# Regrouping the small products of the late steps in a fused linear-attention and feed-forward kernel

## The chip, the core and the metric

The kernel is one program on one core of a Trainium2 chip. Times are device microseconds (us) of that core. The engines are named as in the profile: PE (matrix products; PEld is its weight load), DVE (VectorE), ACT (ScalarE), POOL (GpSimd) and SP, which here issues DMAs.

## The reference, cut to what matters

An attention block with a decaying state runs over 768 tokens for 4 sequences of 8 heads of width 48; its output, as 3072 rows of 384, goes through a feed-forward block of width 2048. Everything is float32.

```python
for t in range(S):
    cur = einsum('bhd,bhe->bhde', u[None] * kt, vt)
    y[:, :, t] = einsum('bhd,bhde->bhe', rt, state + cur)
    state = wt[:, :, :, None] * state + einsum('bhd,bhe->bhde', kt, vt)
...
h = x @ w_in
sp = maximum(h, 0) + log1p(exp(-abs(h)))
return (h * erf(sp)) @ w_out
```

## The kernel before, in words

**Steps.** The kernel takes the tokens in 12 steps, numbered 0 to 11: six chunks of 128 tokens by two halves of the batch. A step holds 2 sequences by 8 heads, and a chunk of 128 tokens is two halves of 64 (`HC`). Steps 0 to 4 are handled by `attend_first` and `attend`. Steps 5 to 11, the late steps (`s > DIRECT`, `DIRECT` is 4), are handled by `attend_late` (L693), and the change is there.

**What a late step computes.** Inside a half of 64 tokens the attention is a triangle of 64 by 64 per head, called `own`. Its blocks of 16 by 16 on the diagonal come from element-wise products and sums on DVE and POOL, made one step ahead by the generator `prepare` (L354). The rest comes from PE at levels 5 and 6, which join blocks of 16 into 32 and of 32 into 64. What came before the half comes from a state of 48 by 48 per head, which decays from half to half.

**Small products.** These attention products use at most 64 of the 128 rows and columns of the PE array. In a late step `s` they are:

- `from_own` (L575, matmuls at L584), in two calls: `own` of step `s-1` times the values, added into the tile `y`;
- `level_products` (L540, matmuls at L552) for level 5 and then for level 6, into the tile `pp0`;
- `through_state` (L598, matmuls at L610): the state of step `s-1`, added into `y`. ACT then copies `y` to `xT`, the input of the feed-forward block, partly by way of `y3` and a DMA;
- `spread_blocks` (L667, matmuls at L672): turns the decays between blocks of 16 (`over_blocks`), which ACT copies to `few` and two DMAs bring to `spread`;
- `state_part` (L650, matmuls at L659): keys times values, which DVE adds to the state. The keys are first multiplied by `spread` (L718), here called the fade of the keys.

**Large products.** `hidden` (L994, matmuls at L1027) is the first feed-forward product, of step `s-1`. `project` (L1044, L1059) and `project_fast` (L1127, L1142) are the second one, of step `s-3`. Each is a generator that emits one piece at a time. Between them stand softplus and erf on ACT (L983, L987, each behind a table load) and a multiplication on DVE (L992). `blend` (L1102) makes the sums that `project_fast` needs out of copies that ACT makes (L1100).

**Order.** Everything from the first step on is written in the order in which each engine executes it; no scheduler moves it. [...] A late step calls `run(stage, following)` at fixed places, and each stage plays a string of tokens (`USUAL`, with two other sets in `LATE` for steps 5 and 11): `P` and `H` are one piece of `project` or `hidden`; `s`, `ey`, `ep`, `m` are softplus, erf into the tile `y` or into `pp1`, and the multiplication of one chunk; `k..`, `S..` are copies and sums for `blend`; `F` lets `prepare` of the next step go on to its next `yield`; `G` sends a weight sum to POOL; `w` sends one of the DVE sums that the last two steps need.

**`prepare` of a late step.** POOL makes products of decays (L402) and `over_blocks` (L424 to L426). DVE makes the near terms of distances 1 to 4 (L463, L467) and sums them (`sum_up`, L453). POOL then makes the terms of distances 5 to 15 (the first of them goes into the room that holds distance 1, so it can start only once that was summed). DVE sums these. Keys and sums are written to DRAM and read back in another layout (`k_blocks` L499, `by_blocks` L501, `by_tokens` L503, `kT` L509), all issued on SP in this order. DVE scales r and k at L328 (`scale`), and at last writes `own` from `by_tokens` (L514), which the next step's first PE instruction reads.

**The queue at the end of a late step.** On DVE, the state sums are `middle` (L736) and, after a POOL product `faded[1]` (L739), `S_next` (L743).

Of the kernel before, what the change touches and what calls it, by code (L numbers as in the profile page):

```python
# [11 lines left out]
FP32 = mybir.dt.float32  # L12
# [5 lines left out]
P = 128  # L18
FAST = 3
EP = 64  # L20
HC = 64
# [40 lines left out]
def kernel(  # L62
# [50 lines left out]
    over_blocks = const.tile([P, C // NEAR, JP], FP32, name="over_blocks")  # L113
# [90 lines left out]
    def near_log(s):  # L204
        return NEAR_LOG - (s == DIRECT)
# [148 lines left out]
    def prepare(s):  # L354
# [61 lines left out]
        if s == DIRECT:  # L416
            yield
        else:
            half = view(tots[NEAR_LOG + 1], 1, [[2, NC], [C >> NEAR_LOG + 1, JP]])
            quarter, last = (  # L420
                view(tots[NEAR_LOG], n, [[4, NC], [C >> NEAR_LOG, JP]]) for n in (1, 3)
            )
            to = over_blocks[:].rearrange("p (h b) n -> p b h n", h=NC)
            nc.gpsimd.tensor_mul(to[:, 0], quarter, half)  # L424
            nc.gpsimd.tensor_copy(out=to[:, 1], in_=half)
            nc.gpsimd.tensor_copy(out=to[:, 2], in_=last)  # L426
            yield
# [84 lines left out]
        scale(s, near_log(s))  # L512
        nb = HC // NEAR
# [153 lines left out]
    def spread_blocks(s, pp):  # L667


        n = D // 2  # L670
        for e in range(NE):
            nc.tensor.matmul(  # L672
                pp[:EP, e, 0:2, HC // 2 : HC // 2 + n],
                lhsT=over_blocks[rows(e)].rearrange("p b n -> p (b n)"),
                rhs=ident[rows(e), rows(e)], start=True, stop=True,
            )
        few = att.tile([EP, NE * 2, n], FP32, name="few", bufs=1)
        nc.scalar.copy(
            few[:].rearrange("p (e i) d -> p e i d", e=NE),
            pp[:EP, :, 0:2, HC // 2 : HC // 2 + n],  # L680
        )
# [3 lines left out]
            in_=few[:].rearrange("p i d -> p (i d)"),  # L685
# [7 lines left out]
    def attend_late(s, run):  # L693
# [10 lines left out]
        take_level(own, pp, LOG - 1)  # L704
        run("front", None)
        if before:
            from_own(before, ready[before][0], 0)
            through_state(before, xTs[before])
            if s + 1 < n_steps:
                load_step(s + 1)  # L710
        following = prepare(s + 1) if s + 1 < n_steps else iter(())
# [3 lines left out]
        run("near", None)  # L715
        next(following, None)
        kT = kTs[s]
        nc.vector.tensor_mul(  # L718
            kT[:].rearrange("p (e n) d -> p n e d", e=NE),
            kT[:].rearrange("p (e n) d -> p n e d", e=NE), spread[s][:],  # L720
        )
        run(0, following)

        pp = products([P, NE, JP, HC], 0)
        level_products(pp, RK, LOG)
        if s + 1 < n_steps:
            spread_blocks(s + 1, pp)
        take_level(own, pp, LOG)
        scale(s, LOG)
        run(1, following)  # L730
        ps = products([P, NC, JP, HC], 0)
        ps = [[ps[:, h]] * NE for h in range(NC)]
        state_part(s, kT, ps)
        run(2, following)
        for e in range(NE):
            nc.vector.tensor_add(middle[rows(e)], faded[0][rows(e)], ps[0][e][rows(e), :, :D])  # L736
        run(3, following)
        if s < n_steps - SPC:
            nc.gpsimd.tensor_mul(  # L739
# [4 lines left out]
        run(4, following)  # L744
# [575 lines left out]
    def in_order(s, k):  # L1320
# [3 lines left out]
        for what in order[k]:  # L1324
# [11 lines left out]
            "s ey", "m", "s ep m P P s ey m P P P", "s P F ep m P F P k22y k11p F", "S1",  # L1336
            "S2 S3 H k12y S4 H F", "s H ep m H H F G s H H H ep",
        ),
        n_steps - 1: (
            "s P", "m w", "ey P m s P P ep P", "m P P", "", "", ""  # L1340
# [3 lines left out]
        "s P", "m", "ey P m s P P ep P", "m k22y P F P k11p F F", "S1", "S2 S3 H k12y S4 H F",  # L1344
        "s H ey m H H F s H ep H H",
# [67 lines left out]
    with tc.manual_schedule(  # L1413
# [77 lines left out]
        run_late(s - 1, "S Q w w w")  # L1491
# [105 lines left out]
```

## Time and profile before

| what | value |
|---|---|
| median of 3 runs | 583.61 us (583.38 to 589.66) |
| profiled execution, its own time | 586.88 us |
| span in its profile | 585.1 us |
| PE busy / DVE / ACT / POOL | 576.4 / 454.7 / 355.6 / 274.1 us |
| late steps 6 to 10, from one first small product to the next | 44.75, 44.50, 44.50, 44.50, 44.49 us |
| granted PE clock | 0.999 |

A busy time of PE counts overlapping matmuls and modelled ends, so that 99% busy isn't 99% of its peak. In the views of the timeline a line is: start in us, length in us, engine, source line, operation, tiles written and read, shape, number of instructions, and in brackets how long the engine stood idle before it and what released it. Each float32 matmul of the program shows as two records on PE. The first small product of step s (L584 for s from 6 to 11) is called A(s) in this text.

### The profile page before, as it was taken

The page shows a single profiled execution, that of the slowest core. Times are in us where ns is not written, and L with a number is a line of the kernel's source. Part 1 is how long each engine was busy: PE and PEld are TensorE (multiplying, and loading weights), DVE is VectorE, ACT ScalarE, POOL GpSimd, SP SyncE. Part 2 cuts the span into 40 slices and gives each one's busy share as a digit, 9 for nine tenths or more (in the row PEclk, how much of TensorE's full clock was granted, in tenths as well). Part 3 has the DMA queues.
Part 4 walks back from the last instruction along what each step waited for, and adds up shares of the span by engine and source line. Part 5 has one row for each costly group of instructions (what it writes and reads, how often), then busy time and mean ns, then how long its engine had stood idle before and what let it go on. Part 6 is the DMA issues. An engine that isn't in the chain of part 4 may idle for free.

```text
span 585.1 us, 16663 instructions
## 1 busy us (share of the span) xinstructions
PE 576.4 (99%) x7240; PEld 495.1 (85%) x7240; DVE 454.7 (78%) x558; ACT 355.6 (61%) x478; POOL 274.1 (47%) x313
## 2 busy tenths in 40 slices
PE   8899999999999999999999999999999999999997
PEld 6588887688668758998898898898898899988997
DVE  6776886999996899799799799799799637256630
ACT  3658877644544598756766666665765771387700
POOL 4557391702398469659459459449549200000000
PEclk9999999999999999999999999999999999999999
DMA  8587571440433414334334334334331301000000
GB/s 269 177 273 281 201 235 44 183 154 10 145 95 116 117 55 156 63 116 165 74 111 169 74 108 172 75 108 136 74 108 55 74 8 36 2 0 2 28 27 29
DMA packets 54082, 63.25 MB, mean 108 GB/s; under 512 B 35160, under 2 KB 40568, under 8 KB 52984
## 3 DMA queue, kind: packets, MB, share of 16 engines
q1 hardware_dynamic: 53624, 61.98, 33.4%
q8 instruction: 57, 0.93, 0.6%
q10 hardware_dynamic: 384, 0.20, 0.1%
q14 instruction: 17, 0.14, 0.1%
HBM read 52.39 MB, written 8.69 MB: 104 GB/s over the span
## 4 chain that ended last, share of the span: by engine, by line
PE 95%; DVE 3%; issue 1%; ACT 0%; POOL 0%; DVEq 0%; POOLq 0%
PE m L1027 36%; PE m L1142 28%; PE m L1059 8%; PE pp L552 6%; PE pp L1230 4%; PE y L1230 2%; PE y L584 2%; PE pp L659 2%; PE y L610 2%; PE m L862 1%; PE pp L871 1%; PE pp L938 1%; DVE in L328 1%; DVE words L467 1%; PE pp L1142 0%
## 5 line engine op out<-in xcount | busy, mean ns | idle before, releaser
L1027 PE MATMUL m<-xT,w_in_sb 128*128 128x256 f32 x960 | 215.3, 382 | 0.1
L1027 PEld LDWEIGHTS m<-xT,w_in_sb 128*128 128x128 f32 x960 | 179.9, 190 | 26.2 <-issue 1.0
L328 DVE TENSOR_TENSOR in<-in,tot_sb 128x1024 f32<-128x1024 f32 (+1 forms) x55 | 75.3, 1369 | 16.5 <-PE pp L552 13.2
L463 POOL TENSOR_TENSOR rk<-words 128x528 f32<-128x528 f32 (+3 forms) x28 | 42.5, 1517 | 91.2 <-DVE sums L453 80.7
L1036 ACT COPY h<-m 128x512 f32<-128x512 f32 x80 | 46.4, 579 | 57.6 <-PE m L1027 57.5
L467 POOL TENSOR_TENSOR words<-words,rest 128x528 f32<-128x528 f32 (+10 forms) x77 | 78.1, 1015 | 6.0
L1059 PE MATMUL m<-w_out_sb,h 128*128 128x384 f32 x192 | 64.3, 491 | 0.0
L1059 PEld LDWEIGHTS m<-w_out_sb,h 128*128 128x128 f32 x192 | 35.7, 190 | 23.5
L1142 PE MATMUL m<-mixed,h 128*128 128x192 f32 x256 | 45.6, 331 | 0.0
L1142 PE MATMUL m<-w_out_sb,h 128*128 128x192 f32 x256 | 44.8, 329 | 0.0
L552 PEld LDWEIGHTS pp<-in 48*64 48x64 f32 (+1 forms) x2368 | 33.4, 126 | 12.0 <-issue 6.2
L1142 PEld LDWEIGHTS m<-mixed,h 128*128 128x128 f32 x256 | 41.4, 190 | 0.9
L1142 PEld LDWEIGHTS m<-w_out_sb,h 128*128 128x128 f32 x256 | 41.6, 190 | 0.3
L1142 PE MATMUL m<-w_out_sb,room 128*128 128x192 f32 x240 | 41.5, 326 | 0.0
L983 ACT ACT_TABLE_LOAD x30 | 38.5, 1283 | 2.7 <-issue 2.2
L987 ACT ACT_TABLE_LOAD x30 | 38.5, 1283 | 1.5 <-DVE room L1125 1.1
L1142 PEld LDWEIGHTS m<-w_out_sb,room 128*128 128x128 f32 x240 | 39.4, 190 | 0.0
L402 POOL TENSOR_TENSOR tot_sb<-tot_sb 128x256 f32<-128x256 f32 (+4 forms) x50 | 36.2, 724 | 3.8
L552 PE MATMUL pp<-in 48*64 48x32 f32 (+1 forms) x2368 | 37.3, 212 | 0.6 <-DVE in L328 0.5
L463 POOL TENSOR_TENSOR words<-words 128x336 f32<-128x336 f32 (+6 forms) x49 | 35.3, 720 | 3.8
L453 DVE TENSOR_REDUCE sums<-rk 128x14 f32<-128x672 f32 (+9 forms) x54 | 34.7, 701 | 0.0
L453 DVE TENSOR_REDUCE sums<-words 128x6 f32<-128x288 f32 (+8 forms) x66 | 26.9, 464 | 3.9 <-POOL words L463 3.6
(198 smaller groups left out, 951.5 us busy)
## 6 DMA issues: line engine op xcount, KB each, us to landing
in<-in_rkw SPq DMA_DIRECT2D x8, 1024.0 KB, 5.1
words<-in_moe_w_in SPq DMA_DIRECT2D x16, 384.0 KB, 5.4
words<-in_moe_w_out SPq DMA_DIRECT2D x16, 384.0 KB, 4.7
words<-in_rk_rows SPq DMA_DIRECT2D x8, 768.0 KB, 5.6
w<-in_rkw SPq DMA_DIRECT2D x11, 512.0 KB
v<-in_v SPq DMA_DIRECT2D x12, 384.0 KB, 5.6
out<-o SPq DMA_DIRECT2D x23, 192.0 KB, 2.4
in<-in_rkw SPq DMA_DIRECT2D x7, 512.0 KB, 5.7
```

What stands on the lines that cost most here:

```text
L328: nc.vector.tensor_mul(halves, halves, view(tots[level - 1], 0, [[1, n], [2, nb], [0, half]]))
L402: nc.gpsimd.tensor_mul(new, pair[:, :, 0], pair[:, :, 1])
L453: nc.vector.tensor_reduce(out=view(sums[:], n, [[near * (NEAR + 1), NEAR // near], [NEAR + 1, near - n]]), in_=terms[n], axis=mybir.AxisLi ...
L463: engine.tensor_mul(terms[n], r[:, :, n:], k[:, :, : near - n])
L467: engine.tensor_mul(k[:, :, :m], k[:, :, :m], w[:, :, n : n + m])
L552: nc.tensor.matmul(to, lhsT=rk(1, n)[rows(e), s0 : s0 + m], rhs=right, start=True, stop=True,)
L983: nc.scalar.activation(sp_room, chunks[0], AF.Softplus)
L987: nc.scalar.activation(at, sp_room, AF.Erf)
L1027: nc.tensor.matmul(ps[:, ff, :], lhsT=w_in_sb[:, g * FG + f + ff, kk * P : (kk + 1) * P], rhs=xT[:, kk, :], start=kk == 0, stop=kk == KT - 1,)
L1036: nc.scalar.copy(h[:, f : f + FT, :], ps[:])
L1059: nc.tensor.matmul(ps[j][:], lhsT=gs[g][:, f, j * C : (j + 1) * C], rhs=w_out_sb[:, g * FG + f, :], start=g + f == 0, stop=g == NG - 1 and ...
L1142: nc.tensor.matmul(to, lhsT=a[:, f], rhs=b[:, f], start=start and f == 0, stop=f == FG - 1, skip_group_check=True,)
```

## The change

**Grouping.** In a late step `s` the small products stand in two groups. The first is unchanged: `from_own(…, 1)` and level 5. The second begins after the stages front and near and holds `from_own(…, 0)`, `through_state`, level 6 and `state_part`, with nothing between them. `state_part` writes to `pp1` where it wrote to `pp0`.

**The key fade.** `fade_keys(s + 1)` is called at the end of step `s`, behind the write of `own`; for step 5 it is called in the step itself, ahead of the stage front.

**The state sums.** They follow the near terms that DVE makes, ahead of the first `sum_up`; `faded[1]` is made on DVE.

**The spread.** `spread_blocks` stands behind stage 0 and is one matmul on the whole array (128 rows, 128 columns of weights, 96 moving columns), for which `over_blocks` has twice its size, the second half staying at 1.0. Step 4 keeps the former form for the spread of step 5.

**Tokens.** In the usual steps the stage near is empty, its `m` being moved to the end of the last stage, and `prepare` has one more `yield`, ahead of the write of `own`, with one more `F` behind that `m`. The other two sets change alike; step 5 keeps its `m` in the stage near. The stage near itself is played ahead of the second group and of `prepare`, where it was behind them.

```diff
@@ prepare
         scale(s, near_log(s))
+        yield
         nb = HC // NEAR
@@ spread_blocks
+        few = att.tile([EP, NE, D], FP32, name="few", bufs=1)
+        if s > DIRECT + 1:
+            got = products([P, NE * JP * HC], 0)[:, : NE * D].rearrange("p (e d) -> p e d", e=NE)
+            nc.tensor.matmul(
+                got, lhsT=over_blocks[:].rearrange("p i b n -> p (i b n)"),
+                rhs=ident[:].rearrange("p (e m) -> p e m", e=NE)[:, :, :D],
+                start=True, stop=True,
+            )
+            nc.scalar.copy(few[:], got[:EP])
...
@@ attend_late
         take_level(own, pp, LOG - 1)
+        if s == DIRECT + 1:
+            fade_keys(s)
         run("front", None)
+        run("near", None)
         if before:
             from_own(before, ready[before][0], 0)
             through_state(before, xTs[before])
             if s + 1 < n_steps:
                 load_step(s + 1)
+        pp = products([P, NE, JP, HC], 0)
+        level_products(pp, RK, LOG)
+        ps = products([P, NC, JP, HC], 1)
+        ps = [[ps[:, h]] * NE for h in range(NC)]
+        state_part(s, kTs[s], ps)
+        take_level(own, pp, LOG)
         following = prepare(s + 1) if s + 1 < n_steps else iter(())
         next(following, None)
         nc.gpsimd.tensor_mul(faded[0][:], S[:], ends[:, :, 0:1].to_broadcast([P, JP, D]))
         next(following, None)
-        run("near", None)
-        next(following, None)
-        kT = kTs[s]
-        nc.vector.tensor_mul(
-            kT[:].rearrange("p (e n) d -> p n e d", e=NE),
-            kT[:].rearrange("p (e n) d -> p n e d", e=NE), spread[s][:],
-        )
-        run(0, following)
-
-        pp = products([P, NE, JP, HC], 0)
-        level_products(pp, RK, LOG)
-        if s + 1 < n_steps:
-            spread_blocks(s + 1, pp)
-        take_level(own, pp, LOG)
-        scale(s, LOG)
-        run(1, following)
-        ps = products([P, NC, JP, HC], 0)
-        ps = [[ps[:, h]] * NE for h in range(NC)]
-        state_part(s, kT, ps)
-        run(2, following)
         for e in range(NE):
             nc.vector.tensor_add(middle[rows(e)], faded[0][rows(e)], ps[0][e][rows(e), :, :D])
-        run(3, following)
         if s < n_steps - SPC:
-            nc.gpsimd.tensor_mul(
+            nc.vector.tensor_mul(
                 faded[1][:], middle[:], ends[:, :, 1:2].to_broadcast([P, JP, D])
             )
             for e in range(NE):
                 nc.vector.tensor_add(S_next[rows(e)], faded[1][rows(e)], ps[1][e][rows(e), :, :D])
-        run(4, following)
+        next(following, None)
+        scale(s, LOG)
+        run(0, following)
+        if s + 1 < n_steps:
+            spread_blocks(s + 1)
+        for n in range(1, 5):
+            run(n, following)
+        for _ in following:
+            pass
+        if s + 1 < n_steps:
+            fade_keys(s + 1)
+
+    def fade_keys(s):
+
+        kT = kTs[s][:].rearrange("p (e n) d -> p n e d", e=NE)
+        nc.vector.tensor_mul(kT, kT, spread[s][:])
@@ tokens
     LATE = {
         DIRECT + 1: (
-            "s ey", "m", "s ep m P P s ey m P P P", "s P F ep m P F P k22y k11p F", "S1",
-            "S2 S3 H k12y S4 H F", "s H ep m H H F G s H H H ep",
+            "s ey", "m", "s ey m P P s ep m P P P", "s P F ep m P F P k22y k11p F", "S1",
+            "S2 S3 H k12y S4 H F", "s H ep m H H F G s H ep H H m F",
         ),
         n_steps - 1: (
-            "s P", "m w", "ey P m s P P ep P", "m P P", "", "", ""
+            "s P", "", "ey P m s P P ep P", "m P P", "", "", ""
         ),
     }
     USUAL = (
-        "s P", "m", "ey P m s P P ep P", "m k22y P F P k11p F F", "S1", "S2 S3 H k12y S4 H F",
-        "s H ey m H H F s H ep H H",
+        "s P", "", "ey P m s P P ep P", "m k22y P F P k11p F F", "S1", "S2 S3 H k12y S4 H F",
+        "s H ey m H H F s H ep H H m F",
     )
...
-        run_late(s - 1, "S Q w w w")
+        run_late(s - 1, "S Q w w w w")
```

More of the change, by code (lines that the diff above doesn't have):

```diff
@@ L111 @@
     seen = const.tile([P, NE * NP * NC], FP32, name="seen")
-    over_blocks = const.tile([P, C // NEAR, JP], FP32, name="over_blocks")
+    over_blocks = const.tile([P, 2, C // NEAR, JP], FP32, name="over_blocks")
     u_sb = const.tile([P, NP], FP32, name="u_sb")
@@ L422, in prepare @@
             )
-            to = over_blocks[:].rearrange("p (h b) n -> p b h n", h=NC)
+            to = over_blocks[:, 0].rearrange("p (h b) n -> p b h n", h=NC)
             nc.gpsimd.tensor_mul(to[:, 0], quarter, half)
@@ L665, in state_part, with spread_blocks @@
                     )
-    def spread_blocks(s, pp):
-        n = D // 2
-        for e in range(NE):
+    def spread_blocks(s, pp=None):
+        few = att.tile([EP, NE, D], FP32, name="few", bufs=1)
+        if s > DIRECT + 1:
+            got = products([P, NE * JP * HC], 0)[:, : NE * D].rearrange("p (e d) -> p e d", e=NE)
             nc.tensor.matmul(
-                pp[:EP, e, 0:2, HC // 2 : HC // 2 + n],
-                lhsT=over_blocks[rows(e)].rearrange("p b n -> p (b n)"),
-                rhs=ident[rows(e), rows(e)], start=True, stop=True,
-            )
[L677 to L680, printed above, removed]
-        )
+                got, lhsT=over_blocks[:].rearrange("p i b n -> p (i b n)"),
+                rhs=ident[:].rearrange("p (e m) -> p e m", e=NE)[:, :, :D],
+                start=True, stop=True,
+            )
+            nc.scalar.copy(few[:], got[:EP])
+        else:
+            n = D // 2
+            got = pp[:EP, :, 0:2, HC // 2 : HC // 2 + n]
+            for e in range(NE):
+                nc.tensor.matmul(
+                    got[:, e], lhsT=over_blocks[rows(e), 0].rearrange("p b n -> p (b n)"),
+                    rhs=ident[rows(e), rows(e)], start=True, stop=True,
+                )
+            nc.scalar.copy(few[:].rearrange("p e (i d) -> p e i d", i=2), got)
         g_rows = dram.tile([C // NEAR, JP * NE * D], FP32, name="g_rows")
@@ L684, in spread_blocks @@
             out=g_rows[:].rearrange("b (n d) -> (b n) d", n=JP),
-            in_=few[:].rearrange("p i d -> p (i d)"),
+            in_=few[:].rearrange("p e d -> p (e d)"),
         )
@@ L714, in attend_late @@
         next(following, None)
-        run("near", None)
-        next(following, None)
-        kT = kTs[s]
-        nc.vector.tensor_mul(
-            kT[:].rearrange("p (e n) d -> p n e d", e=NE),
-            kT[:].rearrange("p (e n) d -> p n e d", e=NE), spread[s][:],
-        )
-        run(0, following)
-        pp = products([P, NE, JP, HC], 0)
-        level_products(pp, RK, LOG)
-        if s + 1 < n_steps:
-            spread_blocks(s + 1, pp)
-        take_level(own, pp, LOG)
-        scale(s, LOG)
-        run(1, following)
-        ps = products([P, NC, JP, HC], 0)
-        ps = [[ps[:, h]] * NE for h in range(NC)]
-        state_part(s, kT, ps)
-        run(2, following)
         for e in range(NE):
             nc.vector.tensor_add(middle[rows(e)], faded[0][rows(e)], ps[0][e][rows(e), :, :D])
-        run(3, following)
         if s < n_steps - SPC:
-            nc.gpsimd.tensor_mul(
+            nc.vector.tensor_mul(
                 faded[1][:], middle[:], ends[:, :, 1:2].to_broadcast([P, JP, D])
```

## The prediction

> **What bounds the kernel now.** I read the chain that ended last first, then the timeline of step 7 (285.73 to 330.23), then that of step 5. The page gives PE nearly everything:
>
> ```profile
> PE 576.4 (99%) x7240; PEld 495.1 (85%) x7240; DVE 454.7 (78%) x558; ACT 355.6 (61%) x478; POOL 274.1 (47%) x313
> ...
> PE 95%; DVE 3%; issue 1%; ACT 0%; POOL 0%; DVEq 0%; POOLq 0%
> ```
>
> So whatever holds PE back is paid in full. Step 7 on PE alone shows the price of changing between large and small products:
>
> ```profile
> 290.02 0.67 PE L584 MATMUL y<-own,v 64*48 64x64 f32 x32
> ...
> 291.51 2.87 PE L1142 MATMUL m<-mixed,h 128*128 128x192 f32 x16
> 294.22 2.76 PE L1142 MATMUL m<-w_out_sb,room 128*128 128x192 f32 x16
> 296.82 2.76 PE L1142 MATMUL m<-mixed,room 128*128 128x192 f32 x16
> 299.42 2.76 PE L1142 MATMUL m<-w_out_sb,room 128*128 128x192 f32 x16
> 302.11 0.76 PE L552 MATMUL pp<-in 48*32 48x32 f32 x64
> ```
>
> Start to start, a large product between large ones takes 2.60 us; behind a small group 2.71; ahead of one 2.69; in the same view one with small groups on both sides 2.79. A group costs 0.2 us beside its work.
>
> The same step on all engines shows a second loop as long as PE's:
>
> ```profile
> 297.94 2.37 DVE L453 TENSOR_REDUCE sums<-rk 128x15 f32<-128x720 f32 x3
> 298.91 1.31 POOL L463 TENSOR_TENSOR rk<-words 128x528 f32<-128x528 f32 x1 [14.23 <-DVE sums L453]
> ...
> 308.42 1.86 POOL L463 TENSOR_TENSOR rk<-words 128x384 f32<-128x384 f32 x1
> ...
> 322.52 0.33 SPq L499 DMA_DIRECT2D k_blocks<-words  x1
> 322.96 0.36 SPq L501 DMA_DIRECT2D by_blocks<-sums  x1
> ...
> 328.67 1.29 DVE L514 TENSOR_TENSOR own<-block_sb,by_tokens 128x1024 f32<-128x1024 f32 x1 [1.84 <-DMA by_tokens<-by_blocks]
> 330.22 0.52 PEld L584 LDWEIGHTS y<-own,v 64*48 64x48 f32 x32 [0.33 <-DVE own L514]
> ```
>
> POOL is idle 14.23 us for the first DVE sum, then works without a pause to 322.5; k_blocks is issued when it ends, by_blocks behind it, by_tokens lands at 328.67, `own` ends at 329.96, and PE's next small product starts at 330.23, when the last large one ends as well (96 records from 309.31). DVE's 1.84 us idle is a flight time, not slack. What moves POOL's start later moves the step's end.
>
> Step 5 is the same loop, begun by DVE at 199.36:
>
> ```profile
> 199.36 0.95 DVE L470 TENSOR_TENSOR words<-words,u_row 128x768 f32<-128x768 f32 x1
> 199.79 1.28 ACT L983 ACT_TABLE_LOAD   x1 [2.21 <-issue]
> 203.46 1.03 ACT L987 ACTIVATE y<-room 128x1024 f32<-128x1024 f32 x1
> 207.05 1.22 DVE L992 TENSOR_TENSOR h<-h,y 128x1024 f32<-128x1024 f32 x1
> 209.16 1.30 POOL L463 TENSOR_TENSOR rk<-words 128x528 f32<-128x528 f32 x1 [11.52 <-DVE sums L453]
> ```
>
> Here the first `m` (L992) comes behind the near terms, long after its erf (to 204.49).
>
> [...] POOL's 384-element product takes 1.86 us beside DVE's L328 and 1.01 at 220.53; the key fade takes 1.72 beside POOL and 0.96 in step 11, where POOL is idle. [...] these go by SP, and take 2.3 (by_blocks) and 3.0 (by_tokens) from issue to landing. [...]
>
> **The change, part by part.** A is the step's first small product.
>
> *Groups.* Steps 6 to 10 lose two each; step 11 loses one (its state products already adjoined the next group); in step 5 three become one, two less. 13 x 0.2 = 2.6 us less PE work. The whole-array spread: 0.25 us of small matmuls become two records of 96 columns, between 0.16 (half of what two of 192 columns take, 2 x 0.16) and 0.33: zero net. A usual step's PE work falls from 44.50 to 44.1.
>
> *Fade.* At the step's end, behind `own`, with POOL done: 0.96 for 1.72. kT's packets end about 2.2 us after by_tokens', so it starts some 2.05 us after `own` starts and ends near A+1.5. DVE's next scale waits for PE until A+1.64, `seen` goes between: nothing, hidden by that idle. Should kT land 1 us later, each step pays about 1.
>
> *State sums* (steps 6 to 10). Near terms end at A+11.1. PE's second group ends at A+7.2 (4.3, plus 2.94 for 0.49, 0.45, 0.45, 0.69, 0.87), so no wait. `middle` 1.14, `faded[1]` on DVE, not seen there: from 0.45 (half of L470's 0.94) to 0.83 (POOL's own time); I take 0.55, as `S_next` per half. `S_next` 1.14. That is 2.8 where an `m` of 1.13 stood: the first sum is 1.7 later and POOL starts at A+14.9, not 13.2. The POOL product and its hop were hidden by DVE's sums; their removal gains nothing.
>
> *POOL's run.* Before: 21.9 us busy, of which 17.6 uncontended and 4.3 waits for DVE. The fade's wait (0.58) leaves, but scales on DVE now meet POOL in other places: gain 0 to 0.9, I take 0.3. POOL ends 1.4 later, at A+38.2. From POOL's end to `own`'s end it took 7.45 to 7.7 (k_blocks, by_blocks 0.44 behind, by_tokens 2.3, landing 3.3, 1.3). `own` ends at A+45.75, PE would be ready at 44.1.
>
> *What else is queued there.* The `m` of the last erf stands ahead of `own`: that erf ends at A+42.3, m to 43.5, `own` could end at 44.8; +0.3 for a step even if POOL lost nothing. On ACT, L569 (1.16) now stands ahead of the first erf; the copies L1153 and L1156, which PE needs two products later, keep 2 us. [...] behind it k12y and the copies L1036 come 1.5 later, where H had 1.2 us in hand: PE stalls about 1.3 inside H, too, an alternative to waiting for `own`, not a sum. The spread's two DMAs keep their place on SP and have 25 us. The state products in `pp1` make the next `ep` wait for `S_next` (A+13.9); it comes at 17.
>
> So a usual period is 45.75 us: 1.0 over step 6's 44.75 and 1.25 over 44.50 four times: **+6.0 us**. From below, 0.3 each; from above, 2.
>
> *Step 5.* PE does level 5 and then level 6 and state at once: level 6 must wait for scale and own (to 199.4), state for the fade (200.3). PE idles 2.3 us. On DVE the `m` now stands ahead of the near terms: DVE is free at 200.3 and waits for the erf until 204.49. Queued behind it: all near terms, then POOL. Near terms start at 205.6 instead of 199.36, end at 213.3; sums of state 2.8; first sum 216.1; POOL at 217.1 instead of 209.16, its run 23.4; end 240.5; `own` at 247.8, A of step 6 at 247.9 against 240.98: **+6.9 us**, PE's own 1.9 inside it. ACT and the copies of H lead to 247.5 to 248.1 by another way (the third erf waits for `S_next` in `pp1`, 216.2). Bounds 5.5[...] and 8.
>
> *Step 11 and the tail.* One group, -0.25. Four `w` at the end for three: 1.2 us of DVE, hidden; their first reader is PE's L1230 at 504.86, the sums end at 498.96.
>
> Sum: 6.9 + 6.0 - 0.25 = 12.65. The profiled execution took 586.88 (span 585.1 and 1.8 around it): 599.5. It lies 3.3 over the median of 583.61; the same step on that gives **596.3 us**.
>
> **The rivals.** (a) *PE's bound holds* and the change does what it says: 583.61 - 2.6 = 581.0, not slower. One mechanism: the loop by POOL and DMA has slack that the trace hides. It decides from 1.7 us of slack a step and 7 in step 5. For: PE has 95% of the chain and PEld waits for `own` only 0.33 at a time. Against: every group boundary shows 0.23 to 0.33 of that sort, and in step 6, where `own` ended latest (A+44.79), the period was 44.75, not 44.50. (b) *Step 5 alone loses*; the later loops keep up[...]: 583.61 + 6.9 - 5 x 0.4 - 0.25 = 588.3. (c) *The fade becomes a bound*: kT lands 1 us later, DVE starts each step late, and the loop grows: 596.3 + 5 = 601.3.
>
> **How the numbers follow.** A measurement of this kernel can tell about 1% (5.8 us) from no change. Forecast 0.63, (a) 0.08, (b) 0.17, (c) 0.12. The forecast's own bounds are 5.5 + 1.25 - 0.25 = 6.5 (590.1) to 8 + 9.75 - 0.25 = 17.5 (601.1). The range drops (a) and the far end of (c): 587.5 to 602. Slower by over 1% (above 589.4): 0.63, (c) and a third of (b): 0.80. Within 1%: most of (b) and (a): 0.18. Faster: 0.02, if groups cost PE more than their starts show.
>
> **What would show it.** Periods between first small products of 45.5 to 46 us in steps 6 to 10 and 51 to 52 from step 5's to step 6's; DVE idle about 4 us ahead of step 5's first L992 multiplication; POOL's first near term at A+14.9; PE idle ahead of L584 or in L1027; a fade of 0.96. Wrong if POOL starts later and `own` still comes in time, or if the fade waits beyond A+1.6.

## The result, and the profile after

The changed kernel takes 600.75 us (median of 6 runs, 598.75 to 602.33); the kernel before, on the same chip, 584.90 us (583.38 to 589.66). The ratio is 1.0261, 95% interval 1.0217 to 1.0304: **slower by 2.6%**. The profiled execution took 601.3 us with a span of 599.5 (before: 586.88 and 585.1). From the added `yield` on, the lines of the code have numbers that are 1 to 10 higher than before: L584 became L585, L552 L553, L610 L611, L659 L660, L514 L515, L1027 L1037, L1142 L1152, L1059 L1069, L992 L1002.

The page of the kernel after: busy time, granted clock of PE, and the chain that ended last.

```profile
PE 582.1 (97%) x7228; PEld 500.6 (84%) x7228; DVE 459.3 (77%) x563; ACT 355.8 (59%) x478; POOL 265.1 (44%) x308
...
PEclk9999999999999799999999989999999989999999
...
PE 55%; DVE 8%; issue 2%; ACT 1%; ACTq 0%; DVEq 0%
```

PE has 12 records fewer than before, and its share of the chain fell from 95% to 55%. Three slices of the clock are below 9 where late steps lie: PE ran at half clock there (granted clock 0.5), for 6.83 us in step 5 (197.21 to 204.04) and for 3.41 us each in steps 8 and 11 (from 347.40 and from 483.93). All six executions of the changed kernel had a granted clock of 0.986 to 0.994.

The table shows where the 14.4 us between the two spans went, step by step in us, by the starts of the first small products A(s). A second profile of the unchanged kernel (`e0_before`) stands beside them, since the first one began step 5 two us late. Step 5 is counted from its first level-5 product.

| step | before | `e0_before` | after |
|---|---|---|---|
| start of step 5, at | 196.14 | 194.20 | 194.13 |
| 5 | 44.84 | 45.67 | 52.39 |
| 6 | 44.75 | 44.50 | 45.59 |
| 7 | 44.50 | 44.50 | 46.01 |
| 8 | 44.50 | 44.50 | 47.82 |
| 9 | 44.50 | 44.50 | 45.22 |
| 10 | 44.49 | 44.49 | 44.07 |
| 11 | 23.15 | 23.15 | 26.04 |
| rest | 98.23 | 98.44 | 98.20 |

Step 5 lost 6.7 us by the second profile (the steps before it end alike); the old order of step 5 takes 44.77 to 45.77 us in the seven traces that have it. Steps 6 to 9 lost 0.7 to 3.3 each, in no regular way; step 10 **gained** 0.4; step 11 lost 2.9.

Step 7 on PE, after (start, length, both in us; in brackets the idle time and its releaser):

```profile
297.90 0.76 PE L553 MATMUL pp<-in 48*32 48x32 f32 x64
298.58 0.75 PE L660 MATMUL pp<-v,kT 64*48 64x48 f32 x47
300.86 0.42 PE L660 MATMUL pp<-v,kT 64*48 64x48 f32 x17 [1.53 <-issue]
301.21 2.87 PE L1152 MATMUL m<-mixed,h 128*128 128x192 f32 x16
```

In the middle of the state products, between the 47th record and the 48th, PE stands for 1.53 us, and the releaser is "issue": it waited for nothing that the profile shows. I call this a hole and count it from start to start, less the usual distance: 1.72 here. Steps 6, 8, 9 and 11 have one of 0.64, 2.07, 1.05 and 1.22 us (that of step 6 comes just behind the group, four records into the large product); step 10 has none. Before, no late step has one. In steps 8 and 11 the half clock follows: in step 11 a large product of 16 records takes 4.55 us, in step 7, at a granted clock of 1.0, 2.87.

Step 5 after, PE, DVE, ACT and POOL:

```profile
197.58 1.08 PE L553 MATMUL pp<-in 48*32 48x32 f32 x64 [2.37 <-DVE own L563]
202.60 1.22 DVE L1002 TENSOR_TENSOR h<-h,y 128x1024 f32<-128x1024 f32 x1 [4.30 <-ACT y L997]
203.73 0.95 DVE L470 TENSOR_TENSOR words<-words,u_row 128x768 f32<-128x768 f32 x1
214.38 1.28 ACT L997 ACT_TABLE_LOAD   x1 [3.64 <-DVE s L738]
215.29 1.31 POOL L463 TENSOR_TENSOR rk<-words 128x528 f32<-128x528 f32 x1 [19.66 <-DVE sums L453]
```

This is what the prediction described: PE idle ahead of level 6, DVE idle for 4.30 us ahead of the multiplication, near terms and POOL late behind it, and the third erf waiting for `S_next`.

The change from step 9 to 10, after:

```profile
431.16 0.66 PE L585 MATMUL y<-own,v 64*48 64x64 f32 x32
431.20 1.23 DVE L515 TENSOR_TENSOR own<-block_sb,by_tokens 128x1024 f32<-128x1024 f32 x1 [0.68 <-DMA by_tokens<-by_blocks]
432.50 0.96 DVE L754 TENSOR_TENSOR kT<-kT,spread 128x768 f32<-128x768 f32 x1
433.37 0.17 DVE L594 COPY seen<-y 128x16 f32<-128x16 f32 x1
433.46 1.22 DVE L328 TENSOR_TENSOR in<-in,tot_sb 128x1024 f32<-128x1024 f32 x1
```

A(10) starts at 431.16, ahead of the write of `own` that it was to wait for. So the forecast's link is not there. At this change of steps `own`, the fade, `seen` and the scale L328 follow one another on DVE without a pause.

### The profile page after: what moved, and what is told of

Its sections match the earlier page's. It is cut to its first block, busy times and chain, and to the rows that moved or that the text cites. A ratio compares the mean times of both kernels' runs of the same rounds, so it can differ in the third digit from the quotient of the medians.

```text
span 599.5 us, 16628 instructions
## 1 busy us (share of the span) xinstructions
PE 582.1 (97%) x7228; PEld 500.6 (84%) x7228; DVE 459.3 (77%) x563; ACT 355.8 (59%) x478; POOL 265.1 (44%) x308
## 3 DMA queue, kind: packets, MB, share of 16 engines
HBM read 52.39 MB, written 8.69 MB: 102 GB/s over the span
## 4 chain that ended last, share of the span: by engine, by line
PE 55%; DVE 8%; issue 2%; ACT 1%; ACTq 0%; DVEq 0%
PE m L1152 25%; PE m L1037 18%; PE pp L1240 4%; PE y L1240 2%; DVE in L328 2%; PE pp L553 2%; PE y L585 1%; DVE sums L453 1%; DVE h L1002 1%; PE y L611 1%; DVE words L467 1%; PE pp L660 1%; DVE rk L463 1%; PE pp L1152 0%; DVE room L1129 0%
## 5 line engine op out<-in xcount | busy, mean ns | idle before, releaser
L1037 PE MATMUL m<-xT,w_in_sb 128*128 128x256 f32 x960 | 216.2, 382 | 1.6 <-ACT h L1046 1.3
L1037 PEld LDWEIGHTS m<-xT,w_in_sb 128*128 128x128 f32 x960 | 179.6, 190 | 29.7 <-ACT h L1046 4.5
L463 POOL TENSOR_TENSOR rk<-words 128x528 f32<-128x528 f32 (+3 forms) x28 | 38.5, 1376 | 113.2 <-DVE sums L453 102.8
L328 DVE TENSOR_TENSOR in<-in,tot_sb 128x1024 f32<-128x1024 f32 (+1 forms) x55 | 81.8, 1488 | 4.4 <-PE pp L553 3.0
L467 POOL TENSOR_TENSOR words<-words,rest 128x528 f32<-128x528 f32 (+10 forms) x77 | 77.4, 1005 | 6.0
L1069 PE MATMUL m<-w_out_sb,h 128*128 128x384 f32 x192 | 66.2, 502 | 0.0
L1069 PEld LDWEIGHTS m<-w_out_sb,h 128*128 128x128 f32 x192 | 36.7, 195 | 24.5 <-issue 1.8
L1152 PE MATMUL m<-mixed,h 128*128 128x192 f32 x256 | 48.5, 345 | 0.5 <-issue 0.5
L553 PEld LDWEIGHTS pp<-in 48*64 48x64 f32 (+1 forms) x2368 | 33.8, 127 | 15.2 <-issue 7.3
L1152 PEld LDWEIGHTS m<-mixed,h 128*128 128x128 f32 x256 | 44.7, 202 | 1.1 <-issue 0.6
L1152 PE MATMUL m<-w_out_sb,h 128*128 128x192 f32 x256 | 44.8, 329 | 0.0
L553 PE MATMUL pp<-in 48*64 48x32 f32 (+1 forms) x2368 | 37.6, 213 | 4.9 <-DVE own L563 2.4
L1152 PEld LDWEIGHTS m<-w_out_sb,h 128*128 128x128 f32 x256 | 41.6, 190 | 0.3
L1152 PE MATMUL m<-w_out_sb,room 128*128 128x192 f32 x240 | 41.5, 326 | 0.0
L1002 DVE TENSOR_TENSOR h<-h,pp 128x1024 f32<-128x1024 f32 x15 | 18.3, 1219 | 29.2 <-ACT pp L997 29.2
L1152 PEld LDWEIGHTS m<-w_out_sb,room 128*128 128x128 f32 x240 | 39.4, 190 | 0.0
```

The source lines that it names most:

```text
L328: nc.vector.tensor_mul(halves, halves, view(tots[level - 1], 0, [[1, n], [2, nb], [0, half]]))
L463: engine.tensor_mul(terms[n], r[:, :, n:], k[:, :, : near - n])
L467: engine.tensor_mul(k[:, :, :m], k[:, :, :m], w[:, :, n : n + m])
L553: nc.tensor.matmul(to, lhsT=rk(1, n)[rows(e), s0 : s0 + m], rhs=right, start=True, stop=True,)
L1037: nc.tensor.matmul(ps[:, ff, :], lhsT=w_in_sb[:, g * FG + f + ff, kk * P : (kk + 1) * P], rhs=xT[:, kk, :], start=kk == 0, stop=kk == KT - 1,)
L1069: nc.tensor.matmul(ps[j][:], lhsT=gs[g][:, f, j * C : (j + 1) * C], rhs=w_out_sb[:, g * FG + f, :], start=g + f == 0, stop=g == NG - 1 and ...
```

## The experiments

Two theories were to be told apart for steps 6 to 11. **L** (loop): the second loop through DVE, POOL and the DMAs sets the period, as forecast. **F** (fetch): PE runs out of instructions in the merged group, which the traces can show only by the places of the holes and of the transfers of instructions. For F speaks a DMA queue of kind "instruction", which brings 16,384 bytes at a time: 57 packets in the kernel before, for 14,480 matmuls and weight loads of PE, so about 254 of these for each packet. In step 7 such a packet starts at 298.26 and the hole ends at 300.86; in steps 8, 9 and 11 the two are 344.60 and 346.98, 391.26 and 393.57, 480.53 and 482.74. In these four steps a hole ends 2.2 to 2.6 us after a packet's start. The merged group holds 448 instructions (224 matmuls and 224 weight loads; 384 in steps 10 and 11, where one half of the state products is left out); in step 6, where the hole comes behind it, it takes 3.04 us (250.81 to 253.85), 6.8 ns an instruction. The longest group of a late step before holds 192.

**The unchanged kernel once more**, with no edit, for a second profile.

> The kernel before once more, to see how far its own step times repeat: steps 6 to 10 at 44.5 to 44.8 each, no hole over 0.5 us in steps 6 to 11, no half-clock spell; step 5 between 44.8 and 46, by how late it begins.

585.74 us, one execution; its periods are in the table above.

**Is the link there? `own` written twice** (the kernel before, the `own` of steps 6 to 11).

```diff
-        nc.vector.tensor_mul(
-            own[:].rearrange("p n (b t) -> p n b t", t=NEAR),
...
+        for _ in range(2 if s > DIRECT + 1 else 1):
+            nc.vector.tensor_mul(
+                own[:].rearrange("p n (b t) -> p n b t", t=NEAR),
...
```

> The kernel before with the write of own (1.2 us on DVE) made twice at the end of steps 5 to 10. The forecast's link (the next step's first small product waits for this write, and both come at the same moment): each of six steps 1.0 to 1.2 us longer, the run 6 to 7 us slower. The rival (the first small product reads the own of the step before; only DVE's next scale stands behind this write, and DVE has about 1.5 us idle there): 0 to 1 us.

584.7 us, ratio 1.0008 (0.9994 to 1.0022); periods 44.50 as before. DVE and PE at the end of step 7:

```profile
326.08 2.65 DVE L515 TENSOR_TENSOR own<-block_sb,by_tokens 128x1024 f32<-128x1024 f32 x2 [1.75 <-DMA by_tokens<-by_blocks]
327.74 0.52 PEld L585 LDWEIGHTS y<-own,v 64*48 64x48 f32 x32 [0.33 <-DVE own L515]
329.39 1.23 DVE L328 TENSOR_TENSOR in<-in,tot_sb 128x1024 f32<-128x1024 f32 x1 [0.57 <-PE pp L553]
```

The two writes end at 328.73, and A starts a us earlier. The forecast's link is false. In the code, A of step s is `from_own(before, ready[before][0], 1)` with `before = s - 1`: it reads the `own` that was written a whole step earlier. (What is said of this in the text ahead of the prediction, and in the first part of the prediction, is wrong.) The bracket "0.33 <-DVE own" names the last event, not a wait: 0.33 stands ahead of every A from step 6 to 11 of the kernel before, whatever the releaser. At A(7) it is "issue", and `own` was still being written:

```profile
284.22 1.55 DVE L514 TENSOR_TENSOR own<-block_sb,by_tokens 128x1024 f32<-128x1024 f32 x1 [1.59 <-DMA by_tokens<-by_blocks]
285.72 0.52 PEld L584 LDWEIGHTS y<-own,v 64*48 64x48 f32 x32 [0.33 <-issue]
```

The write ends at 285.77 and A(7) has begun at 285.72. So the trace before already spoke against the link.

**Moving the instructions' numbers.** 38 small matmuls of no use, 152 instructions, are put at the start of the changed kernel.

```diff
+        extra = ps_m.tile([P, NC, P], FP32, name="m")
+        for _ in range(38):
+            nc.tensor.matmul(
+                extra[:EP, 0, :EP], lhsT=ident[:D, :EP], rhs=ident[:D, :EP], start=True, stop=True,
+            )
```

> The changed kernel with 38 more small matmuls (152 PE instruction records, about 0.6 us) at the very start, nothing else. In the changed kernel PE stands still inside the merged group: 1.7 us in step 7, 2.1 in step 8, 1.05 in step 9, none in step 10, 1.2 in step 11, at a place that moves earlier by 42 to 44 records a step. Theory F (PE runs out of fetched instructions[...]): the block edges move by 152 records, so the holes change steps: none in 7 and 8, about 1 us in step 9 at the group's end, 1.5 to 2 us in steps 10 and 11. Theory D (a data wait: keys, fade, pp1): the holes stay in the same steps at the same sizes, since no wait has changed.

610.11 us, one execution; its early part was 10 us longer, with a spell of half clock, so the time itself says nothing. The holes changed steps: none in the merged groups of steps 7, 8 and 11, one of 0.94 now in step 10, which had none, 1.44 in step 6 and 1.65 in step 9. The products of the late steps and their order are unchanged, so a wait for their data would have left the holes in their places. In detail the forecast was right for steps 7 and 8, right in place for step 9 (1.65 for about 1), too large for step 10 and wrong for step 11. Where in the run of instructions the small products stand matters, then, though the rule that I used for it is not complete.

**Breaking the run of small products.** One large product of the stage behind is put into the middle of the merged group.

```diff
             through_state(before, xTs[before])
+            run_late(s, "P")
...
-        "s P", "", "ey P m s P P ep P", "m k22y P F P k11p F F", "S1", "S2 S3 H k12y S4 H F",
+        "s P", "", "ey m s P P ep P", "m k22y P F P k11p F F", "S1", "S2 S3 H k12y S4 H F",
```

> The changed kernel with one large product put between through_state and level 6 in steps 6 to 11 (taken from stage 0), so that the second group is cut in two. Theory F: no hole over 0.5 us in steps 6 to 11 and no half-clock spell in steps 8 and 11; steps 8 and 11 fall by 3 us each. What steps 6 to 9 then take tells the next thing. If only PE bounds them: 44.2 to 44.4 each, in all 9 to 10 us less than the changed kernel. If the loop over DVE, POOL and the DMAs of the forecast is there as well: 45.3 to 45.9 each, in all 5 to 7 us less. Theory D: holes remain ahead of the state products.

595.43 us, ratio 1.0182 (1.0158 to 1.0206): some 5 us less than the changed kernel, although it has a group more in each step. Step 7:

```profile
295.59 0.63 PE L611 MATMUL y<-in,middle 48*48 48x64 f32 x32
296.15 2.87 PE L1153 MATMUL m<-mixed,h 128*128 128x192 f32 x16
298.95 0.81 PE L553 MATMUL pp<-in 48*32 48x32 f32 x64
299.69 0.94 PE L660 MATMUL pp<-v,kT 64*48 64x48 f32 x64
300.56 2.87 PE L1153 MATMUL m<-w_out_sb,room 128*128 128x192 f32 x16
```

There is no hole in the groups of steps 6 to 11, and no half clock there. A packet of instructions starts at 296.44, and the large product runs until 298.95, 2.51 us later, which is as far behind a packet's start as the holes of the changed kernel end (2.2 to 2.6). Periods: 45.59, 45.05, 45.01, 45.09, 44.89, step 11 23.93, with about 0.4 us a step in a new wait of PE for ACT (a copy of `o`), so not yet the 44.3 that PE's own work gives.

**The same without touching any wait.** In the kernel before, the level-5 products of steps 6 to 11 are issued three times over (same result), which makes its first group 448 instructions long.

```diff
-        level_products(pp, RK, LOG - 1)
+        for _ in range(3 if s > DIRECT + 1 else 1):
+            level_products(pp, RK, LOG - 1)
```

> The kernel before, where level 5 is issued three times over in steps 6 to 11 (the same products into the same places): its first group then is a run of 448 PE instruction records, as long as the merged group of the change, with no wait, no order and no operand changed. Without a limit on fetching: each of the six steps 2.0 us longer (two times 1.02), 12 in all, evenly. With one (theory F): in some of the six steps a hole of 1 to 2 us inside the group or just behind it, at a place that moves from step to step, and none of it where the group is short; perhaps a half-clock spell behind a hole.

598.87 us, one execution. The added products take about 1.9 us a step, which steps 9 and 10 show (46.37, 46.35). Steps 6, 7 and 8 take 47.52, 47.76 and 48.05. Step 7's start:

```profile
285.26 0.66 PE L584 MATMUL y<-own,v 64*48 64x64 f32 x32
285.74 2.48 PE L552 MATMUL pp<-in 48*64 48x32 f32 x156
289.31 0.77 PE L552 MATMUL pp<-in 48*64 48x32 f32 x36 [1.09 <-issue]
```

The hole is there in a kernel that has no part of the change: 1.07, 1.30 and 1.59 us in steps 6, 7 and 8. A packet started at 286.97; the hole ends 2.34 us later. This decides for F as the cause of the holes. Half clock followed none of these three (granted clock of the run 1.0). In the kernel before, which has as many packets (57) as the changed one, no late step has a hole; in the merged group of the changed kernel, or just behind it, the holes are 0.64 to 2.07 us.

**Step 5: the multiplication behind the near terms again.**

```diff
-            "s ey", "m", "s ey m P P s ep m P P P", "s P F ep m P F P k22y k11p F", "S1",
+            "s ey", "", "m s ep m P P s ey m P P P", "s P F ep m P F P k22y k11p F", "S1",
```

> The changed kernel with step 5's first multiplication moved behind the first sums of the near terms (stage near empty, stage 0 begins with m, its erf tiles in the order pp1, y). The forecast's account of step 5 (DVE idle 4.3 us for an erf, everything behind it late): near terms start about 5.5 us earlier, POOL's run too, step 5 falls from 52.5 to 46.5 to 48 us, the run by 4 to 6 us. If instead PE's idle ahead of level 6 and its half-clock spell set step 5: it falls by less than 1 us.

595.25 us, ratio 1.0200 (1.0146 to 1.0254). POOL starts at 208.78 in place of 215.29, as expected, but step 5 falls only to 50.33, not to 46.5 to 48. The changed order of step 5 takes 51.42 to 52.39 in three traces (`after`, `e1_shift`, `e2_split`), so the gain is 1.1 to 2.1 us. The time fell by 5.5 us, inside the 4 to 6 that were expected, but in good part by luck: in this trace no hole of steps 6 to 11 was followed by half clock. What is late next in step 5 is PE's own side:

```profile
226.86 2.46 PEld L1037 LDWEIGHTS m<-xT,w_in_sb 128*128 128x128 f32 x12 [0.91 <-ACT h L1046]
229.81 2.46 PEld L1037 LDWEIGHTS m<-xT,w_in_sb 128*128 128x128 f32 x12 [0.49 <-ACT h L1046]
```

PE still idles 2.36 us ahead of level 6, a half clock follows, and in H the weight loads stand idle for ACT's copies, which costs PE 0.67 and 0.25 us.

**Step 5: two large products ahead of the merged group as well.**

```diff
-            "s ey", "m", "s ey m P P s ep m P P P", "s P F ep m P F P k22y k11p F", "S1",
+            "s ey P P", "", "m s ep m P s ey m P P", "s P F ep m P F P k22y k11p F", "S1",
```

> The changed kernel with two edits in step 5 alone: its first multiplication stands behind the near terms as in the run before this one, and two large products stand between level 5 and level 6. If the step's loss is both (DVE waiting for the erf, and PE idle 2.6 us ahead of level 6 with a half-clock spell after it), it is now gone: step 5 45 to 46.5 us for 52.4, no PE hole over 1 us there, the run 6 to 7 us less than the changed kernel and 2 less than with the multiplication alone. If something else set it (the keys' fade, the state sums): step 5 stays over 48.

599.81 us, ratio 1.0208 (1.0153 to 1.0263); step 5 takes 51.41, a miss by 5 us. The idle time ahead of level 6 is gone, and a larger one has come later:

```profile
220.78 0.46 ACT L1078 COPY o<-m 128x384 f32<-128x384 f32 x1
...
221.29 2.64 PEld L1037 LDWEIGHTS m<-xT,w_in_sb 128*128 128x128 f32 x7 [4.33 <-ACT o L1078]
```

PE had used up its large products and waits for ACT's copy, which stands behind an erf that waited 2.82 us for DVE. In steps 7 to 9 all three holes (1.67 to 1.74) were now followed by half clock, and those periods are 47.4 to 47.6. Step 7 of the changed kernel, with a hole of 1.72 and no half clock, took 46.01.

**Both mended**: the last edit, and a large product ahead of level 6 in steps 6 to 11.

```diff
+            run_late(s, "P")
...
-        "s P", "", "ey P m s P P ep P", "m k22y P F P k11p F F", "S1", "S2 S3 H k12y S4 H F",
+        "s P", "", "ey P m s P ep P", "m k22y P F P k11p F F", "S1", "S2 S3 H k12y S4 H F",
```

> Both mends together: step 5 as in e5_step5, and one large product ahead of level 6 in steps 6 to 11, with the token P of stage 0 ahead of s so that ACT's copy for it isn't behind a softplus. Three groups a step in place of four. If instruction fetch and step 5 are all that the change lost: steps 6 to 10 at 44.3 to 44.5 each, the run within 2 us of the kernel before. If the loop over DVE, POOL and DMA binds as well: steps 6 to 9 at 45 to 45.9, the run 3 to 6 us slower than before.

593.53 us, ratio 1.0133 (1.0102 to 1.0163). There are no holes and no half clock from step 6 to 11, and yet steps 6 to 9 take 45.06, 45.02, 45.02 and 45.05; step 10, which has no `faded[1]` and no `S_next` on DVE, takes 44.26. Something of the kind of L is left when the holes are gone. The table of waits from 245 to 425 (total us, times, longest) has this row, where the kernel before has 0.4 us, once:

```profile
PEld m L1038 <- ACT h L1047: 4.6, 12, 0.4
```

H, 96 records, lasts 21.6 us in steps 6 to 9 and 20.88 in step 10: the whole excess of 0.75 lies within H, where those waits are.

**ACT's blend copy behind the second piece of H**, on top of the last.

```diff
-        "s P", "", "ey P m s P ep P", "m k22y P F P k11p F F", "S1", "S2 S3 H k12y S4 H F",
+        "s P", "", "ey P m s P ep P", "m k22y P F P k11p F F", "S1", "S2 S3 H H k12y S4 F",
```

> The kernel with one large product between the first part of the merged group and level 6 (and step 5 in its second arrangement), with one further edit: in steps 6 to 10 ACT's copy for the blend (k12y) is issued behind the second piece of H, not behind the first. There PE waited up to 0.4 us at a time for ACT's copies of H, which stand behind k12y, and k12y waits for DVE's first sum. If this is what holds steps 6 to 9 at 45.02, the H of 96 records falls from 21.63 to 20.9 us, the periods to 44.3, and the time from 593.5 to 590.5 us. If another part of the loop (POOL, DMA, own, the scale on DVE) holds 45.0, PE waits elsewhere and the periods stay at 44.9 to 45.1, 593.5 us.

591.73 us, ratio 1.0120 (1.0103 to 1.0137). Only step 6 gained (44.50); steps 7 to 9 stay at 44.97 to 45.00, with PE waiting in other places (the first wait in H is gone, others and a wait for DVE's sum of `o` remain). The copy is where PE notices the loop, not what holds it.

**Step 5 as before, the rest as changed.** A function of its own, `attend_fifth`, plays step 5 behind level 5 in the order of the kernel before, with the old form of the spread for step 6.

```diff
+        if s == DIRECT + 1:
+            attend_fifth(s, pp, run)
+            return
...
-            "s ey", "m", "s ey m P P s ep m P P P", "s P F ep m P F P k22y k11p F", "S1",
+            "s ey", "m", "s ep m P P s ey m P P P", "s P F ep m P F P k22y k11p F", "S1",
```

> Step 5 alone as before: level 5, its own stages, the first near terms ahead of the erf's multiplication, fade and level 6 and state products apart, the state sums at their old places; all other steps as changed. If the order inside step 5 costs what the forecast gave it, the period of step 5 falls from 52.39 to 45 to 46 us, POOL's first near term comes at about 13 to 15 us after level 5 and not 21, and the time is 600.75 - 6.7 = 594 us; the holes in the merged groups of the later steps stay, in size (1 to 2 us), though they may change steps, so 592 to 596. If instead the loss of step 5 came from what the step makes for step 6 (keys faded at its end, multiplication ahead of own), the period stays above 49 us and the time above 598.

591.1 us, ratio 1.0109 (1.0090 to 1.0129). Step 5 takes 44.77 and POOL starts at 206.65, 13.0 us after level 5: all of step 5's loss came from the order inside it. The holes stayed (1.21, 1.75, 1.87, 1.32, none, 1.77). The median is 9.65 below the changed kernel's, 2 more than step 5 gives. The rest fits the spells of half clock: the profiled execution has three of them and took 595.16 us, another with a granted clock of 0.994 took 595.21, and the four at 1.000 took 589.87 to 591.40, while no execution of the changed kernel was above 0.994.

**Everything mended**: step 5 as before, a large product ahead of level 6, the copy behind the second H. Against the changed kernel:

```diff
+        if s == DIRECT + 1:
+            attend_fifth(s, pp, run)
+            return
...
+            run_late(s, "P")
...
-        "s P", "", "ey P m s P P ep P", "m k22y P F P k11p F F", "S1", "S2 S3 H k12y S4 H F",
+        "s P", "", "ey P m s P ep P", "m k22y P F P k11p F F", "S1", "S2 S3 H H k12y S4 F",
```

> Both edits together: step 5 as before, one large product between the first part of the merged group and level 6, k12y behind the second piece of H. What is left of the change are four small groups made three, the early state sums and the late fade. If the parts add, step 5 takes 45.7, steps 6 to 10 44.26 each and step 11 23.3: 290.3 against 291.3 us in the kernel before, 583.9 us, ratio 0.998. If the second loop still holds steps 6 to 9 at 45.0 it is 586.9, ratio 1.003. If holes come back, 1 to 2 us for each step that has one.

585.9 us, ratio 1.0023 (1.0008 to 1.0039): the second case of the expectation. Step 5 44.77, then 44.86, 45.04, 44.99, 45.03, 44.27, 23.32. DVE from the end of step 7 into step 8, A(8) being at 328.68:

```profile
328.05 1.23 DVE L515 TENSOR_TENSOR own<-block_sb,by_tokens 128x1024 f32<-128x1024 f32 x1 [0.25 <-DMA by_tokens<-by_blocks]
329.87 0.96 DVE L792 TENSOR_TENSOR kT<-kT,spread 128x768 f32<-128x768 f32 x1 [0.60 <-DMA kT<-k_blocks]
330.75 0.17 DVE L594 COPY seen<-y 128x16 f32<-128x16 f32 x1
330.83 1.21 DVE L328 TENSOR_TENSOR in<-in,tot_sb 128x1024 f32<-128x1024 f32 x1
```

The fade waits for the keys to land, ends 2.15 us after A, and DVE goes on into the scale and the near terms with no idle time. Before, DVE waited for PE ahead of that scale (0.74 us). So there seems to be a ring without PE in it: keys land, fade, scale, near terms, state sums, first sum, POOL, keys written and read back.

**The state sums behind the near terms' sums**, on top of the last, to shorten that ring.

```diff
+        next(following, None)
         for e in range(NE):
             nc.vector.tensor_add(middle[rows(e)], faded[0][rows(e)], ps[0][e][rows(e), :, :D])
...
-        next(following, None)
         scale(s, LOG)
```

> The kernel with both edits together, with one more: in steps 6 to 11 the state sums stand behind the sums of the near terms on DVE, not ahead of the first, so that POOL's near terms start 2.8 us earlier in the step; keys are still faded at the step's end. If steps 6 to 9 are held at 45.0 by a ring that leaves PE out (keys land, fade, seen, the scale L328, near terms, state sums, first sum, POOL's run, keys written and read back), the ring is 2 us or more shorter: POOL starts at 12.6 to 13.4 us behind A in place of 15.4, DVE waits for PE again ahead of the scale, the periods fall to 44.26 to 44.5 and the time from 585.9 to 583 or 584, ratio 0.997 to 1.000. If what holds 45.0 is DVE's own length up to the first blend sum (PE waits for ACT's copies of H behind it), nothing is gained: POOL starts earlier, the periods stay at 44.9 to 45.1, 585.9 us.

587.08 us, ratio 1.0058 (1.0037 to 1.0080): no gain; the periods of steps 7 to 9 stay at 44.95 to 44.99. But they come about in another way:

```profile
331.15 1.23 DVE L328 TENSOR_TENSOR in<-in,tot_sb 128x1024 f32<-128x1024 f32 x1 [0.19 <-PE pp L553]
...
349.22 1.28 ACT L1035 ACT_TABLE_LOAD   x1 [3.62 <-DVE s L741]
...
353.58 20.59 PEld L1075 LDWEIGHTS m<-xT,w_in_sb 128*128 128x128 f32 x96 [0.74 <-DVE o L1210]
```

POOL started 12.1 us behind A instead of 15.4, DVE waits for PE again ahead of the scale, and H lasts 20.99: the ring is open. In exchange `faded[1]`, which now runs beside POOL, takes 1.45 us for 0.56, the erf in `pp1` waits for `S_next`, the multiplication and the sum of `o` come later behind it, and PE loses about 0.6 us a step ahead of H. So the ring is not the only thing at 45.0, and what it costs by itself is not shown; which order of DVE would let PE have its 44.26 stayed open. None of these kernels beats the one before.

## Why the prediction was right, and where it was not

The time was forecast as 596.3 and measured as 600.75, slower by over 1%, inside the range. The direction was right, and the loss of step 5 was foreseen with its main causes. The loss of steps 6 to 10 has the size that was forecast, but mostly another cause, so the number is better than the reasons. Of the 4.45 us between forecast and measurement about 1.3 are the base (584.90 for 583.61) and 3.1 are step 11.

- **Groups, 0.2 us each**: right. Step 10 is free of holes and waits and has two groups fewer: 44.07 for 44.49. With one group fewer (`e6_mended`) it takes 44.26.
- **DVE and POOL to the end of the step**: nearly right. In steps 7 to 9 POOL begins at A+14.95 (forecast 14.9), and in steps 7 and 9 it ends at A+37.8 (38.2); `faded[1]` takes 0.56 (0.55), the fade 0.95 to 0.96. That 4.3 us of POOL's 21.9 are waits for DVE was the author's estimate from products that take longer beside DVE's L328 (L467 at 128x384: 1.86 at 310.36 in the profile before, 1.01 at 220.53); the trace shows the lengths, not what made them longer. Where no hole disturbs it and POOL starts at the same place (`e6_mended`), `own` ends at A+45.3 to A+45.5 (45.75).
- **"`own` ends at A+45.75, PE would be ready at 44.1"**, and so a period of 45.75: **this step failed**. A doesn't read that `own` (`e4_own2`). The prediction had noted that each group's edge shows 0.23 to 0.33 and still took the releaser named beside it for a wait. It even has the counter-example: in step 6 `own` ended at A+44.79 and the next A came at A+44.75, before it.
- **The fade "hidden by that idle", over by A+1.5**: right at the starts of steps 7 to 9 of the changed kernel (A+1.19 to A+1.56), wrong at those of steps 10 and 11 (A+2.30 and A+2.40), one of the two signs that it gave of being wrong. In `e10_all`, without holes, the fade is over at A+2.1 to A+2.7 in every step, and DVE's next scale stands behind it. That is the mechanism of rival (c), without a later landing of kT (1.82 us from `own`'s start to the fade's, forecast 2.05). What this costs alone is not shown, since the periods stay at 45.0 where the ring is open (`e11_sums`). In `e6_mended` the 0.75 us of a step show as waits of H for ACT's copies, which the prediction gave as the other way of losing time (about 1.3); the way by `own` had 1.65.
- **Not in the prediction at all**: the holes in and behind the merged group, which the runs put down to PE's supply of instructions. In steps 6 to 9 the changed kernel loses 0.64 + 1.72 + 2.07 + 1.05 = 5.5 us in holes, about 1.7 in the half clock of step 8, and 1.05 in H's waits in steps 6 and 7 (H lasts 21.76 and 21.05 for 20.88), less 2.1 for ten groups: 6.1. Measured over steps 6 to 10: 6.2 against `e0_before`. The forecast's +6.0 is the same size **by coincidence**. Of the periods that were to show it, 45.5 to 46 us, two of five came (45.59 and 46.01), and the holes are in neither of the places where it looked for PE's idle time. In steps 8 and 9, behind holes of 2.07 and 1.05, H takes 20.88 and has no such waits; that a PE which is late by a hole finds ACT's copies ready is a likely reason, not a tested one.
- **Step 5, +6.9**: right in size (6.7 against `e0_before`), and in what was to be seen: idle time of PE ahead of level 6 2.4 (2.3), DVE's wait 4.30 (about 4). Two paths carry it, as the prediction said in its last sentence on it; taking one away (`e3_m5`) gives back 1.1 to 2.1 us, undoing the whole order (`e8_old5`) 6.7 to 7.6. The half clock of 6.8 us behind PE's idle time was not forecast, and its part in the loss was not separated.
- **Step 11, -0.25**: failed, +2.9: a hole of 1.22 and about 1.7 of half clock. Nor is the saving of a group seen there: `e5_step5` takes 24.63 with a hole of 1.49 and no half clock, so 23.14 without the hole, and the kernel before 23.15.
- **Rivals**: (a) is refuted by the time. (b), the late loops keep up, comes close to what the mended kernels show, where 0.5 us a step are lost, but not to the kernel as changed. (c) forecast 601.3, which is nearer to 600.75 than the prediction's number, and it has a place where DVE does start late; but the 1 us a step that it adds is not what the changed kernel lost, so this is luck too.

So the terms that failed in the sum are the period of 45.75 (through `own`) and the -0.25 of step 11; what stands in place of both is mainly the holes, and the half clock behind two of them.

## What to carry to other kernels

Putting small matmuls together saved 0.2 us here for each group (step 10: 44.07 for 44.49, with two groups fewer). But runs of 384 and 448 instructions at 6.8 to 7.9 ns each had holes in them or just behind them in five of the six steps of the changed kernel, of 0.64 to 2.07 us, and runs of 192, at 7.8 ns, had none; with a large product in between (`e2_split`, `e6_mended`) the holes were gone. Suspect the supply of instructions where "issue" idle stands in the middle of a run of equal matmuls. A releaser in brackets is the last event, not the proof of a wait: see whether the reader has ever begun before the write ended, ask the code which buffer is read, or double the supposed cause. When an operation is moved into idle time at the end of a step, add up the whole chain behind it on that engine in the state after the change, not in the one before.

## What the runs showed of the hardware

- From the end of the hole of step 6 of the changed kernel to that of step 7 PE begins 1025 instructions (matmuls and weight loads), from step 7 to 8 1023, from step 8 to 9 1025, and four packets of 16,384 bytes start in each of the three stretches: 256 instructions for each packet. A step has 1067 on PE (steps 6 to 9), which is 4 x 256 + 43. The hole moves towards the front of the group by 21 or 22 matmuls and as many weight loads in each step (behind the 47th, 25th and 4th record of L660 in steps 7, 8 and 9): the remainder. The five holes of the changed kernel end 2.21 to 2.60 us after a packet starts (step 6: 253.03 and 255.25), that of step 7 of `e7_long` 2.34; the transfer itself takes 0.93 to 1.40 for these five packets. What sets when a packet starts is open; in step 10 of the changed kernel it came at 434.86 (A+3.7), and there was no hole.
- After some holes (2.07 and 1.22 us in the changed kernel, steps 8 and 11) PE ran at half clock: 16 records took 4.55 for 2.87. The granted clock of the changed kernel changes at 197.21, 204.04, 347.40, 350.81, 483.93 and 487.34: 6.83, 143.36, 3.41, 133.12 and 3.41 us apart, which is 2, 42, 1, 39 and 1 times 3.413. A spell of 3.41 cost 1.68 us in step 8 (47.82, less the hole of 2.07, less step 10's 44.07) and 1.67 in step 11 (26.04, less the hole of 1.22, less the 23.15 of the kernel before).
- Why some holes have half clock behind them and others not is not shown. In the changed kernel PE stands from 345.10 to 346.98 in step 8 and from 481.70 to 482.74 in step 11, and half clock begins at 347.40 and 483.93. It stands from 299.33 to 300.86 in step 7, longer than in step 11, with no half clock behind it; in step 7 of `e5_step5` a hole of much the same size (1.67 to 1.74 in its steps 7 to 9) was followed by it. So the size of a hole alone doesn't decide it.
